# Joined copies and sums over pairs of PSUM banks in a SwiGLU stage on one Trainium2 core

## The chip, the cores and the metric

The kernel runs on one core of one Trainium2 chip. Times are device microseconds (us) of one execution. The profile counts its span from the first to the last instruction, which is a few microseconds less than the device time. Engines: PE is TensorE (matmul; PEld its weight load), ACT is ScalarE, DVE is VectorE, POOL is GpSimd, SP issues most DMAs.

## The reference

Two blocks follow one another, in float32. The first is an attention with sketched features, for 4 batches, 4 heads, 1088 positions and a head size of 32:

```python
def phi(x):
    a = np.einsum('rd,bhsd->bhsr', S1, x)      # r = 8
    b = np.einsum('rd,bhsd->bhsr', S2, x)
    return np.einsum('bhsi,bhsj->bhsij', a, b).reshape(*x.shape[:-1], r * r)
q_p, k_p = phi(q), phi(k)
kv = np.einsum('bhsf,bhsd->bhfd', k_p, v)
z = np.sum(k_p, axis=2)
num = np.einsum('bhsf,bhfd->bhsd', q_p, kv)
den = np.einsum('bhsf,bhf->bhs', q_p, z)[..., None] + 1e-06
```

Its result `num / den`, with the heads laid side by side, is `x` of 4352 tokens by 128. The second block is `g = x @ w_gate`, `silu(g) * (x @ w_val) @ w_out`, with 1536 hidden columns.

## The kernel before, in words

**Tiling.** The tokens lie transposed in `xT` (128 rows, 4352 columns), cut into 12 blocks, three to a batch, of 384, 384 and 320 columns. The hidden columns are 12 chunks of 128. A *unit* `(i, j)` is block `i` and chunk `j`: a gate product, a value product, Silu of the gate, and their product `hj` in one slot of `hbuf`. A *down* product (`down`, L943) then adds `wo` of that chunk times `hj` into the block's accumulator bank, and after the twelfth the block is transposed (`store`, L972) and sent out. The list `todo` keeps the down products five or six units behind.

**Full and cut products.** A full float32 product (L912 in `unit`, L880 for a gate) goes through TensorE in two passes. The units of batches 1 to 3 replace it by three cheaper products of parts (`cut_unit`). Each weight chunk and each token block is split into a coarse part, a scaled fine part and a difference: `w1`, `wb`, `wd` and `x1`, `x0`, `xd` (`cut_weights` L849, `cut_tokens` L859, L860, L864). The product is

```python
d = wd @ xd                                # one bank          L878
p = w1 @ x1 + wb @ x0                      # a second bank     L884, L885
s = (1 + 1/BETA) * p - d / BETA            # ACT L890, then DVE L893
```

The copy on ACT (L890) brings `-d / BETA` from PSUM into an SBUF tile `sum`, and one DVE operation (L893) adds the scaled `p` in place. In a unit with `both` false only the value product is made of parts, and the gate is a full product. In a unit with `both` true gate and value both are: two `d`, two `p`, two L890, two L893, one Silu (L897) that reads the gate's sum, and one GpSimd product (L902).

**Order.** The kernel is written under a manual schedule: each engine runs its instructions in the order in which the code gives them out, and waits on semaphores where data or a buffer isn't there. For a unit of both, ACT's order is copy, copy, Silu, and then the next unit's.

**Stages.** After a head (sketches, batch 0's attention, 36 full units of batch 0, and the first parts of the weights) comes the main loop over `y`, 108 units in the order of `line`: blocks 3, 4, 5, 6, 7, 8, 9, 11, 10, twelve units each, so 384 columns for `y` 0 to 23, 320 for 24 to 35, and so on. Units from `GATES` (22) on are of both; the last unit is a plain `unit`. Between units `parts_of` advances a generator, `attentions()`, which prepares the next batches' attention in pieces. `GROUPS` (6, 8, 22, 24, 40) are the units before which its TensorE pieces run: the numerators of a batch (L760, with copies L777 on ACT and DVE), its key-value sums (L370, and L698 for the key sums `zs`), and the key and query sketches (L336, L324, with copies L572).

**Key sums.** `feature_sums` gives four GpSimd steps (L529) that add up the key features of a batch. For the third batch they were dealt out between the steps of `turn_keys` and `turn_queries` by `beside`, one each.

**Banks.** PSUM has eight banks, `PS`. In the main loop `bank()` takes the one that was used longest ago, except bank 3 (`acc`), which is held for the accumulators. `wide("a")` and `wide("b")` are banks 4, 5 and 6, 7.

Of the kernel before, what the change touches and what calls it, by code (L numbers as in the profile page):

```python
# [7 lines left out]
FP32 = mybir.dt.float32  # L8
# [11 lines left out]
def kernel(  # L20
# [89 lines left out]
    def bank(tag=None):  # L110

        if tag is not None:
            i = place[tag]
        elif oldest[0]:
            i = min((i for i in used if i not in held), key=used.get)
        else:
            i = place[free_banks[turn[0] % len(free_banks)]]
            turn[0] += 1
        touch(i)
        return PS[:, i, :]  # L120

    def wide(tag):
        i = place[tag]
# [418 lines left out]
    def beside(gen, steps):  # L542

        for x in gen:
            if steps:
                steps.pop(0)()
            yield x
# [49 lines left out]
    def attentions():  # L597

        yield from turn_keys(1)
        yield from turn_queries(1)
        hold("a")
        kp = wide("a")
        for i, c in enumerate(kpieces):
            key_products(kp[:, i, :], *c)
        ka = apool.tile([P, NC * H, R], FP32, tag="kas", name="kas")

        def sketch(ps, i):
            c0, c1 = kpieces[i]  # L610
            return ps[:, i, 0 : 64 * (c1 - c0)].rearrange("p (x t r) -> p x t r", t=2, r=R)

        for i, (c0, c1) in enumerate(kpieces):
            nc.scalar.copy(ka[:, H * c0 : H * c1, :], sketch(kp, i)[:, :, 0, :])
        phk = apool.tile([P, NC, H, R, R], FP32, tag="phk", name="phk")
        for n, (i, c0, c1) in enumerate(((0, 0, 3), (0, 3, 5), (1, 5, 7), (1, 7, 9))):
            first = H * (c0 - kpieces[i][0])
            kb = sketch(kp, i)[:, first : first + H * (c1 - c0), 1, :]
            key_features(phk, (ka[:, H * c0 : H * c1, :], kb), c0, c1)
            if n == 3:  # L620
                release("a")
            if n % 3 != 1:
                yield
        zs, sums = feature_sums(phk)
        for f in sums:
            f()
        yield from turn_keys(2)
        kvz = wide("a")
        values(kvz[:, 0, :], phk, zs)
        kab, kcopies = sketched(wide("b"), key_products, 2, "kab2")  # L630
        fold(kvz[:, 0, :])
        spread = spread_out(1, kvz[:, 0, :])
        hold("a", "b")
        yield
        qab, copies = sketched(wide("a"), query_sketches, 3, "qab")
        run_copies(copies, 2)
        yield
        run_copies(kcopies, 2)
        release("a", "b")
        for n, _ in enumerate(query_step(1, qab)):  # L640
            if n % 2 == 0:
                yield
        yield
        yield
        numerators(1, spread)
        yield "first"

        phk = apool.tile([P, NC, H, R, R], FP32, tag="phk", name="phk")
        yield from features(phk, kab)
        zs, sums = feature_sums(phk)  # L650
        yield from beside(turn_keys(3), sums)
        yield from beside(turn_queries(2), sums)
        for b in (2, 3):
            yield "pe"
            if b == 3:
                numerators(2, spread)
            hold("a")
            kv = bank()
            release("a")
            values(kv, phk, zs)  # L660
            if b == 2:
                kab, copies = sketched(wide("a"), key_products, 2, "kab2")
                run_copies(copies, 2)
            fold(kv)
            spread = spread_out(b, kv)
            yield
            yield "pe"
            qab, copies = sketched(wide("b"), query_sketches, 3, "qab")
            run_copies(copies, 2)
            yield  # L670
            if b == 2:
                yield from turn_queries(3)
                phk = hbuf[:, NH - 6 :, :].rearrange("p s (n h i j) -> p (s n) h i j", h=1, i=R, j=R)
                phk = phk.rearrange("p (c h) o i j -> p c (h o) i j", h=H)
                yield from features(phk, kab)
                zs, sums = feature_sums(phk)
            yield from beside(query_step(b, qab), sums)
        yield "pe"
        numerators(3, spread)
        yield  # L680
# [170 lines left out]
    def cut_tokens(i, engine=nc.gpsimd):  # L851
# [14 lines left out]
            op0=ALU.mult, op1=ALU.add,  # L866
        )

    def cut_unit(i, j, both=False):

        t0, n = blocks[i]
        x1, x0, xd = (x[:, 0:n] for x in x_parts[i])
        ws = (wg, wv) if both else (wv,)
        parts = [[x[:, j % 3, :] for x in w_parts[id(w), j // 3]] for w in ws]
        ds = [bank()[:, 0:n] for _ in ws]
        g = None if both else bank()[:, 0:n]
        for d, (_, _, wd) in zip(ds, parts):
            nc.tensor.matmul(d, wd, xd, start=True, stop=True)  # L878
        if not both:
            nc.tensor.matmul(g, wg[:, j, :], xT[:, t0 : t0 + n], start=True, stop=True)  # L880
        ps = []
        for w1, wb, _ in parts:
            p = bank()[:, 0:n]
            nc.tensor.matmul(p, w1, x1, start=True, stop=False)  # L884
            nc.tensor.matmul(p, wb, x0, start=False, stop=True)  # L885
            ps.append(p)
        sums = []
        for d in ds:
            s = fpool.tile([P, BW], FP32, tag="sgl", name="sum", bufs=6)[:, 0:n]
            nc.scalar.activation(s, d, AF.Copy, scale=-1.0 / BETA)  # L890
            sums.append(s)
        for p, s in zip(ps, sums):
            nc.vector.scalar_tensor_tensor(  # L893
                out=s, in0=p, scalar=1.0 + 1.0 / BETA, in1=s, op0=ALU.mult, op1=ALU.add
            )
        sg = fpool.tile([P, BW], FP32, tag="sg", name="sg", bufs=5)[:, 0:n]
        nc.scalar.activation(sg, sums[0] if both else g, AF.Silu)  # L897
        slot_of[i, j] = slots.pop(0)
        hj = hbuf[:, slot_of[i, j], :]
        hidden[i, j] = hj  # L900
        todo.append((i, j))
        nc.gpsimd.tensor_tensor(out=hj[:, 0:n], in0=sg, in1=sums[-1], op=ALU.mult)  # L902

    def unit(i, j, late=False, between=(None, None)):


        t0, n = blocks[i]
        g, u = bank(), bank()
        for o, w in ((g, wg), (u, wv)):
            if between[0] and w is wv:  # L910
                between[0]()
            nc.tensor.matmul(  # L912
                o[:, 0:n], w[:, j, :], xT[:, t0 : t0 + n], start=True, stop=True
            )
        sg = fpool.tile(
            [P, BW], FP32, tag="sgl" if late else "sg", name="sg", bufs=6 if late else 5
        )
        nc.scalar.activation(sg[:, 0:n], g[:, 0:n], AF.Silu)  # L918
        slot_of[i, j] = slots.pop(0)
        hj = hbuf[:, slot_of[i, j], :]  # L920
        hidden[i, j] = hj
        todo.append((i, j))
        if late:
            if between[1]:
                between[1]()
            nc.scalar.copy(hj[:, 0:n], u[:, 0:n])
            lates.append((hj[:, 0:n], sg[:, 0:n]))
        else:
            nc.vector.tensor_tensor(  # L929
                out=hj[:, 0:n], in0=sg[:, 0:n], in1=u[:, 0:n], op=ALU.mult  # L930
            )
# [213 lines left out]
    for z, (i, j) in enumerate(seq):  # L1145
# [16 lines left out]
        if z == 20:  # L1162
            lows = [
                pool.tile([P, 3, P], FP32, tag=tag, name="low", bufs=bufs)[:]
                for pool, tag, bufs in ((apool, "qb", 2), (apool, "dT", 2), (apool, "rd", 2), (fpool, "sgl", 6))
            ]
            first, low, second, third = cut_weights(wv, lows, nc.gpsimd)
        if z in (20, 21):
# [29 lines left out]

    line = [3 * b + k for b in range(1, B) for k in ((0, 2, 1) if b == B - 1 else range(3))]
    END = len(line) * NCH  # L1200
    GROUPS, GATES = (6, 8, 22, 24, 40), 22

    token_steps = {}
    for m, i in enumerate(line[1:], 1):
# [7 lines left out]
    for y in range(END):  # L1212
        i, j = line[y // NCH], y % NCH
        if y in GROUPS:
            group()
        if y == END - 1:
            unit(i, j)
        else:
            cut_unit(i, j, both=y >= GATES)
        for _ in range(2):  # L1220

            if len(todo) > min(5 + (todo[0][1] == 0), END - y + 1):
                down()
        parts_of(y < GATES or y % 2 == 0)
        if y == 0:
            gate_rows = cut_weights(wg, lows, nc.vector)
        for n, row in enumerate(gate_rows):
            if y >= (0, 1, 5, 5)[n]:
                take(row, 1)
        for gen in token_steps.get(y, ()):  # L1230
            next(gen, None)
# [43 lines left out]
```

## Time and profile before

| | us |
|---|---|
| device time, median of 3 runs | 293.69 (293.32 to 293.71) |
| span of the profiled run | 289.9 |
| PE busy | 280.7 (97%) |
| DVE busy | 207.1 (71%) |
| ACT busy | 181.5 (63%) |
| POOL busy | 162.7 (56%) |
| down products L943, 288 | 103.0 |
| copies L890, 192 of them | 80.4 |
| sums L893, 192 of them | 93.9 |
| Silu L897, 85 that read a sum | 42.7 |

The first rows are the whole run, the last four are groups of instructions. "x2" behind a group in the order of time means that two instructions are merged into one line. "Idle before" is an engine's idle time ahead of a group, and the arrow names what ended most of it. The main loop begins at about 92.8 us and the first unit of both has its copies at 140.62 us. The granted clock of TensorE is 1.00 throughout.

### The profile page before, as it was taken

How to read it: one execution, taken by the hardware profiler on the slowest of the kernel's cores; microseconds unless marked ns; L12 is line 12 of the kernel's file. 1: busy time of each engine (PE TensorE's matmuls, PEld its weight loads, DVE VectorE, ACT ScalarE, POOL GpSimd, SP SyncE). 2: the span in 40 equal slices, each digit the busy share in tenths (PEclk: the TensorE clock that was granted, in tenths of full speed). 3: DMA queues.
4: the chain of work that ended last, by engine and by line, in shares of the span. 5: the costliest groups of instructions: out<-in, count | busy, mean ns of one | idle time of the engine just before them, and what ended most of it. 6: DMA issues, size and time to landing. Idle time of an engine off the chain costs nothing.

```text
span 289.9 us, 6382 instructions
## 1 busy us (share of the span) xinstructions
PE 280.7 (97%) x2307; PEld 212.4 (73%) x2307; DVE 207.1 (71%) x422; ACT 181.5 (63%) x432; POOL 162.7 (56%) x183
## 2 busy tenths in 40 slices
PE   8899999999999969999999999999999999999995
PEld 7545566656656657776787768888888888888984
DVE  3997988875677975999578867657666666676651
ACT  3567565732402936564466678887888887888860
POOL 3315322379301794789737665667576665765650
PEclk9999999999999999999999999999999999999999
DMA  7564292312411213001001001001001010010101
GB/s 193 162 209 111 64 308 77 107 49 83 110 18 18 47 65 86 0 1 27 13 6 27 2 0 25 1 0 32 0 0 27 2 24 1 2 27 0 23 2 27
DMA packets 26142, 14.33 MB, mean 49 GB/s; under 512 B 19840, under 2 KB 24192, under 8 KB 26112
## 3 DMA queue, kind: packets, MB, share of 16 engines
q1 hardware_dynamic: 25456, 13.84, 18.4%
q8 instruction: 18, 0.29, 0.4%
q10 hardware_dynamic: 656, 0.10, 0.2%
q14 instruction: 12, 0.10, 0.1%
HBM read 11.41 MB, written 2.23 MB: 47 GB/s over the span
## 4 chain that ended last, share of the span: by engine, by line
PE 84%; DVE 6%; POOL 3%; ACT 2%; issue 2%; DMA 1%; SPq 0%; DVEq 0%; POOLq 0%; ACTq 0%
PE PS L943 26%; PE PS L912 16%; PE PS L884 10%; PE PS L878 10%; PE PS L885 10%; PE PS L880 4%; PE PS L336 2%; PE PS L324 2%; PE PS L760 2%; POOL zs L529 2%; DVE sum L893 1%; DMA kld<-in_k_dram 1%; ACT sum L890 1%; PE PS L370 1%; POOL hbuf L902 1%
## 5 line engine op out<-in xcount | busy, mean ns | idle before, releaser
L902 POOL TENSOR_TENSOR hbuf<-sg,sum 128x384 f32<-128x384 f32 (+1 forms) x107 | 109.4, 1025 | 61.4 <-ACT sg L897 51.2
L893 DVE SCALAR_TENSOR_TENSOR sum<-PS,sum 128x384 f32<-128x384 f32 (+1 forms) x192 | 93.9, 526 | 48.3 <-ACT sum L890 42.1
L943 PE MATMUL PS<-hbuf,wo 128*128 128x384 f32 (+2 forms) x288 | 103.0, 459 | 0.0
L890 ACT ACTIVATE sum<-PS 128x384 f32<-128x384 f32 (+1 forms) x192 | 80.4, 465 | 13.3 <-PE PS L878 12.9
L897 ACT ACTIVATE sg<-sum 128x384 f32<-128x384 f32 (+1 forms) x85 | 42.7, 503 | 27.3 <-DVE sum L893 27.3
L943 PEld LDWEIGHTS PS<-hbuf,wo 128*128 128x128 f32 x288 | 52.0, 189 | 10.3 <-issue 0.4
L878 PE MATMUL PS<-xd,gphq 128*128 128x384 f32 (+1 forms) x85 | 47.9, 564 | 0.0
L884 PE MATMUL PS<-x,w 128*128 128x384 f32 (+1 forms) x107 | 42.2, 394 | 0.1
L878 PE MATMUL PS<-xd,wd 128*128 128x384 f32 (+1 forms) x107 | 39.4, 369 | 0.7 <-DVE sum L893 0.4
L885 PE MATMUL PS<-x,wb 128*128 128x384 f32 (+1 forms) x107 | 35.0, 327 | 0.0
L918 ACT ACTIVATE sg<-PS 128x384 f32<-128x384 f32 (+1 forms) x37 | 17.4, 474 | 22.0 <-PE PS L912 20.3
L912 PE MATMUL PS<-xT,wg 128*128 128x384 f32 (+1 forms) x74 | 29.5, 480 | 0.0
L912 PE MATMUL PS<-xT,wv 128*128 128x384 f32 (+1 forms) x74 | 28.8, 471 | 0.2 <-DVE wv L270 0.2
L878 PEld LDWEIGHTS PS<-xd,wd 128*128 128x128 f32 x107 | 20.3, 189 | 11.5 <-DVE sum L893 1.2
L884 PE MATMUL PS<-x,graw 128*128 128x384 f32 (+1 forms) x85 | 27.9, 328 | 0.0
L885 PE MATMUL PS<-x,graw 128*128 128x384 f32 (+1 forms) x85 | 27.6, 325 | 0.0
L929 DVE TENSOR_TENSOR hbuf<-sg,PS 128x384 f32<-128x384 f32 (+1 forms) x31 | 16.2, 526 | 10.9 <-PE PS L912 10.5
L884 PEld LDWEIGHTS PS<-x,w 128*128 128x128 f32 x107 | 20.1, 188 | 4.2 <-ACT sum L890 0.4
L878 PEld LDWEIGHTS PS<-xd,gphq 128*128 128x128 f32 x85 | 16.1, 189 | 8.6 <-issue 0.4
L885 PEld LDWEIGHTS PS<-x,wb 128*128 128x128 f32 x107 | 20.2, 188 | 2.9
L912 PEld LDWEIGHTS PS<-xT,wv 128*128 128x128 f32 x74 | 13.8, 190 | 9.2 <-DVE hbuf L929 0.9
L912 PEld LDWEIGHTS PS<-xT,wg 128*128 128x128 f32 x74 | 13.3, 189 | 9.3 <-issue 1.2
(130 smaller groups left out, 345.2 us busy)
## 6 DMA issues: line engine op xcount, KB each, us to landing
kld<-in_k_dram SPq DMA_DIRECT2D x4, 544.0 KB, 4.1
vld<-in_v_dram SPq DMA_DIRECT2D x12, 144.0 KB, 4.6
qld<-in_q_dram SPq DMA_DIRECT2D x3, 544.0 KB, 3.3
raw<-in_moe_w_out_dram SPq DMA_DIRECT2D x4, 384.0 KB, 3.8
out_dram<-o SPq DMA_DIRECT2D x28, 48.0 KB, 1.9
raw<-in_moe_w_gate_dram SPq DMA_DIRECT2D x3, 384.0 KB, 3.1
raw<-in_moe_w_val_dram SPq DMA_DIRECT2D x3, 384.0 KB, 3.5
out_dram<-o SPq DMA_DIRECT2D x16, 40.0 KB, 1.7
```

Of the source, the lines that this page charges most:

```text
L878: nc.tensor.matmul(d, wd, xd, start=True, stop=True)
L880: nc.tensor.matmul(g, wg[:, j, :], xT[:, t0 : t0 + n], start=True, stop=True)
L884: nc.tensor.matmul(p, w1, x1, start=True, stop=False)
L885: nc.tensor.matmul(p, wb, x0, start=False, stop=True)
L890: nc.scalar.activation(s, d, AF.Copy, scale=-1.0 / BETA)
L893: nc.vector.scalar_tensor_tensor(out=s, in0=p, scalar=1.0 + 1.0 / BETA, in1=s, op0=ALU.mult, op1=ALU.add)
L897: nc.scalar.activation(sg, sums[0] if both else g, AF.Silu)
L902: nc.gpsimd.tensor_tensor(out=hj[:, 0:n], in0=sg, in1=sums[-1], op=ALU.mult)
L912: nc.tensor.matmul(o[:, 0:n], w[:, j, :], xT[:, t0 : t0 + n], start=True, stop=True)
L918: nc.scalar.activation(sg[:, 0:n], g[:, 0:n], AF.Silu)
L929: nc.vector.tensor_tensor(out=hj[:, 0:n], in0=sg[:, 0:n], in1=u[:, 0:n], op=ALU.mult)
L943: nc.tensor.matmul(acc[i][:, 0:n], wo[:, j, :], hidden[i, j][:, 0:n], start=(j == 0), stop=(j == NCH - 1),)
```

## The change

The change has four parts.

1. A new `pair()` takes two neighbouring banks at once. A unit of both puts its two `d` on one pair and its two `p` on another, so that one ACT copy and one DVE sum of 2 x 384 (or 2 x 320) columns take the place of two each. `doubles` gives the sum tiles: tiles of two halves, four buffers, in place of six single ones. This is for fewer instructions on ACT and DVE.
2. `GATES` goes from 22 to 18: four more units make the gate of parts too. The rate of `parts_of` keeps its limit of 22.
3. The key sums of the third batch are given out in one go, ahead of `turn_keys(3)`, and the first two `GROUPS` come at units 5 and 7 in place of 6 and 8, so that TensorE reaches the values a unit earlier.
4. The gate weights' later rows are cut a unit later, and the fourth low part of the value weights lies in a buffer of tag `qb`, since `sgl` has another shape now.

```diff
+    def pair():
+        i = min((i for i in (0, 4, 6) if i not in held), key=lambda i: max(used[i], used[i + 1]))
+        touch(i, i + 1)
+        return PS[:, i : i + 2, :]
...
         zs, sums = feature_sums(phk)
-        yield from beside(turn_keys(3), sums)
-        yield from beside(turn_queries(2), sums)
+        for f in sums:
+            f()
+        yield from turn_keys(3)
+        yield from turn_queries(2)
...
+    room = [None, 2]
+    def doubles(k):
+        if room[1] + k > 2:
+            room[:] = fpool.tile([P, 2, BW], FP32, tag="sgl", name="sum", bufs=4), 0
+        at = room[1]
+        room[1] += k
+        return room[0][:, at : at + k, :]
...
-        ds = [bank()[:, 0:n] for _ in ws]
+        ds = pair()[:, :, 0:n] if both else bank()[:, 0:n].unsqueeze(1)
         g = None if both else bank()[:, 0:n]
-        for d, (_, _, wd) in zip(ds, parts):
-            nc.tensor.matmul(d, wd, xd, start=True, stop=True)
+        for k, (_, _, wd) in enumerate(parts):
+            nc.tensor.matmul(ds[:, k], wd, xd, start=True, stop=True)
...
-        ps = []
-        for w1, wb, _ in parts:
-            p = bank()[:, 0:n]
-            nc.tensor.matmul(p, w1, x1, start=True, stop=False)
-            nc.tensor.matmul(p, wb, x0, start=False, stop=True)
-            ps.append(p)
-        sums = []
-        for d in ds:
-            s = fpool.tile([P, BW], FP32, tag="sgl", name="sum", bufs=6)[:, 0:n]
-            nc.scalar.activation(s, d, AF.Copy, scale=-1.0 / BETA)
-            sums.append(s)
-        for p, s in zip(ps, sums):
-            nc.vector.scalar_tensor_tensor(
-                out=s, in0=p, scalar=1.0 + 1.0 / BETA, in1=s, op0=ALU.mult, op1=ALU.add
-            )
+        ps = pair()[:, :, 0:n] if both else bank()[:, 0:n].unsqueeze(1)
+        for k, (w1, wb, _) in enumerate(parts):
+            nc.tensor.matmul(ps[:, k], w1, x1, start=True, stop=False)
+            nc.tensor.matmul(ps[:, k], wb, x0, start=False, stop=True)
+        sums = doubles(len(ws))[:, :, 0:n]
+        nc.scalar.activation(sums, ds, AF.Copy, scale=-1.0 / BETA)
+        nc.vector.scalar_tensor_tensor(
+            out=sums, in0=ps, scalar=1.0 + 1.0 / BETA, in1=sums, op0=ALU.mult, op1=ALU.add
+        )
         sg = fpool.tile([P, BW], FP32, tag="sg", name="sg", bufs=5)[:, 0:n]
-        nc.scalar.activation(sg, sums[0] if both else g, AF.Silu)
+        nc.scalar.activation(sg, sums[:, 0] if both else g, AF.Silu)
...
-    GROUPS, GATES = (6, 8, 22, 24, 40), 22
+    GROUPS, GATES = (5, 7, 22, 24, 40), 18
...
-        parts_of(y < GATES or y % 2 == 0)
+        parts_of(y < 22 or y % 2 == 0)
...
-            if y >= (0, 1, 5, 5)[n]:
+            if y >= (0, 2, 6, 6)[n]:
                 take(row, 1)
```

More of the change, by code (lines that the diff above doesn't have):

```diff
@@ L901, in cut_unit @@
         todo.append((i, j))
-        nc.gpsimd.tensor_tensor(out=hj[:, 0:n], in0=sg, in1=sums[-1], op=ALU.mult)
+        nc.gpsimd.tensor_tensor(out=hj[:, 0:n], in0=sg, in1=sums[:, len(ws) - 1], op=ALU.mult)
     def unit(i, j, late=False, between=(None, None)):
@@ L914, in unit @@
             )
-        sg = fpool.tile(
-            [P, BW], FP32, tag="sgl" if late else "sg", name="sg", bufs=6 if late else 5
-        )
+        sg = doubles(1)[:, 0, :] if late else fpool.tile([P, BW], FP32, tag="sg", name="sg", bufs=5)
         nc.scalar.activation(sg[:, 0:n], g[:, 0:n], AF.Silu)
@@ L1164 @@
                 pool.tile([P, 3, P], FP32, tag=tag, name="low", bufs=bufs)[:]
-                for pool, tag, bufs in ((apool, "qb", 2), (apool, "dT", 2), (apool, "rd", 2), (fpool, "sgl", 6))
+                for pool, tag, bufs in ((apool, "qb", 2), (apool, "dT", 2), (apool, "rd", 2), (apool, "qb", 2))
             ]
```

## The prediction

> **What bounds the kernel now.** I read the page's busy line first, then the chain that ended last, then the last stage by form and in order of time.
>
> The busy line and the chain:
>
> ```profile
> PE 280.7 (97%) x2307; PEld 212.4 (73%) x2307; DVE 207.1 (71%) x422; ACT 181.5 (63%) x432; POOL 162.7 (56%) x183
> ...
> PE 84%; DVE 6%; POOL 3%; ACT 2%; issue 2%; DMA 1%; SPq 0%; DVEq 0%; POOLq 0%; ACTq 0%
> ```
>
> The reader is to see that TensorE is busy nearly throughout and owns the end. ScalarE at 63% looks like an engine with room. The next two views show why that is not so.
>
> The groups by form between 175 and 285 us (busy, mean ns, idle before and its releaser):
>
> ```profile
> L893 DVE SCALAR_TENSOR_TENSOR sum<-PS,sum 128x384 f32<-128x384 f32 x86 | 44.0, 553 | 24.0 <-ACT sum L890 23.6
> ...
> L890 ACT ACTIVATE sum<-PS 128x384 f32<-128x384 f32 x86 | 37.2, 485 | 0.3 <-PE PS L878 0.2
> ...
> L897 ACT ACTIVATE sg<-sum 128x384 f32<-128x384 f32 x43 | 22.6, 526 | 12.5 <-DVE sum L893 12.5
> L893 DVE SCALAR_TENSOR_TENSOR sum<-PS,sum 128x320 f32<-128x320 f32 x48 | 21.3, 486 | 11.6 <-ACT sum L890 11.4
> ...
> L890 ACT ACTIVATE sum<-PS 128x320 f32<-128x320 f32 x48 | 18.2, 431 | 0.1
> ```
>
> Each engine of a unit waits for the other: the sums for the copies, the Silu for the sums. The copies wait for almost nothing, so they start when the Silu ahead of them in ScalarE's queue is done.
>
> One turn of that ring, in order of time, where nothing else disturbs it (start, length):
>
> ```profile
> 169.97 0.85 ACT L890 ACTIVATE sum<-PS 128x384 f32<-128x384 f32 x2
> ...
> 170.47 1.02 DVE L893 SCALAR_TENSOR_TENSOR sum<-PS,sum 128x384 f32<-128x384 f32 x2 [0.50 <-ACT sum L890]
> ...
> 171.07 0.52 ACT L897 ACTIVATE sg<-sum 128x384 f32<-128x384 f32 x1 [0.24 <-DVE sum L893]
> 171.50 0.85 ACT L890 ACTIVATE sum<-PS 128x384 f32<-128x384 f32 x2
> ```
>
> First copy to first sum 0.50 us, first sum to Silu 0.60, Silu to the next unit's copy 0.43: 1.53 us a turn. The second copy runs beside the first sum, and the second sum beside the Silu. For 320 columns the same reading (copies at 150.08, sums at 150.53, Silu at 151.06, copies at 151.43) gives 0.45 + 0.53 + 0.37 = 1.35.
>
> TensorE in the steady part, the second difference product of two successive units:
>
> ```profile
> 184.55 0.34 PE L878 MATMUL PS<-xd,wd 128*128 128x384 f32 x1
> ...
> 186.25 0.34 PE L878 MATMUL PS<-xd,wd 128*128 128x384 f32 x1
> ```
>
> That is 1.70 us a unit (six products 0.17 apart and a down product of 0.65). TensorE sets the time with 0.17 us to spare over the ring. This margin is what the change must not use up.
>
> Earlier, the one real hole in TensorE, from the waits between 100 and 106 us:
>
> ```profile
> PE PS L698 <- POOL zs L529: 2.3, 1, 2.3
> ```
>
> The third batch's key sums reach TensorE late.
>
> **What the Trainium skill says.** PSUM — Partial Sum Buffer, section "Engine vs sequencer instructions": the queues of ScalarE, VectorE and GpSimd are strictly first in, first out. The trace agrees: before the Silu at 149.70 ScalarE stood idle for 1.56 us on a sum, with the next unit's copies behind it. ScalarE: Activation LUTs, "What ACT_TABLE_LOAD costs": 186 ns + 0.833 ns per element for an ACTIVATE with immediate scale, successive ones overlapping by about 93 ns. At 384 that is 506 ns against 485 here. VectorE: DVE Perf Modes, section on the TRN2 errata: 120 cycles and one per element from PSUM at 0.96 GHz, 525 ns at 384 against 553 here. So both engines pay mostly per element, and joining two operations saves only the fixed part.
>
> **The change part by part.**
>
> *Joined copies and sums.* No instruction with 768 elements from PSUM is in the trace. From the two widths, L890 costs (485 - 431)/64 = 0.84 ns per column and L893 (553 - 486)/64 = 1.05. So 384 more columns add 0.32 us to the copy (0.81) and 0.40 to the sum (0.95); 320 more add 0.27 and 0.335. The skill's prices give estimates of 0.83 and 0.93 for 768. From above, a joined operation should cost no more than the two that it replaces (0.85 and 1.02). I take 0.81 and 0.95.
> Per unit this saves about 0.04 us of ScalarE and 0.07 of VectorE, but it puts both halves in series. The gate's sum can't start before the value's copy is done, and the Silu can't start before the value's sum is done. The new wait is the Silu's: behind it on ScalarE stands the next unit's joined copy, for which the next sum, and then the PSUM pair, and then TensorE wait. The ring becomes, at 384: 0.50 + 0.32 = 0.82 to the sum, 0.60 + 0.40 = 1.00 to the Silu, 0.43 to the next copy: 2.25 us. At 320: 0.72 + 0.87 + 0.37 = 1.96. TensorE's 1.70 no longer hides it.
>
> *Pairs of banks.* A unit of both takes two of three pairs where seven single banks turned before. The next difference products wait for the sum of two products back, which ended before; the next value products wait for the joined copy. Both come ahead of ScalarE's turn in the ring, so I cost this at nothing: the ring hides it.
>
> *How many turns.* Units 18 to 105 start 88 periods: 52 at 384 and 36 at 320 (blocks of 12 units; 18 to 23 at 384, then 12 at 320, 24 at 384, 12 at 320, and so on): 52 x 2.25 + 36 x 1.96 = 187.6 us.
> To that come ScalarE's other work and TensorE's groups, hidden before and now in the ring: six token copies (L859) at 0.42, 2.5 us; the group at unit 22, where the numerators (1.56 us on TensorE) wait for unit 21's sum, and then values, a copy of 0.70 and the next products follow, 5.35 instead of 2.25, 3.1 us; the query sketches at 24 (1.67 us on TensorE, ScalarE copies of 1.14) 1.2; the denominator chain on VectorE (147.14 to 149.18, five operations, against some 1.1 us free) 0.8; the numerators at unit 40, 2.0; single turns where two other VectorE operations of 0.5 and 0.95 meet, 0.7. In all 10.3 us. Alone, an operation of 0.95 fits in VectorE's gap of 1.1 to 1.3.
> Before, first copy of unit 18 to that of unit 106 took 279.08 - 129.67 = 149.4 us. Change: 187.6 + 10.3 - 149.4 = +48.5 us.
>
> *Gates from 18.* Four units take six short products in place of three and a full gate product. On TensorE that would save 4 x (1.82 - 1.70) = 0.5 us (1.82 is the distance of units at 121 to 128 us). In the ring it costs 4 x 0.43; the +48.5 holds it.
>
> *Key sums at once, groups at 5 and 7.* Before, the sums on GpSimd (1.3, 1.3, 1.0, 0.9 us) stand between units' products and end at 104.1. In one go they start when the third batch's features are done (94.3) and end at about 98.8. A group one unit earlier reaches them after its key products at about 99.9, so the wait of 2.3 us goes. The units' products queue behind the sums, some 2.7 us later at unit 0; their down products come seven units on, which hides that. I take -2.3 us, between -0.5 and -2.8.
>
> *Gate rows a unit later, GATES split from the 22 of the attention parts, another home for the fourth low part, the doubled sum tiles.* Nothing: the rows were done by about unit 10, and the low part's old contents are dead some 10 us before the next tokens are cut.
>
> *Tail.* Before, 10.8 us from unit 106's copy to the end, TensorE with a backlog. After, TensorE has none: 3.4 us to the last GpSimd product, 2.4 of down and last products, 3.4 for copy and transfer out, 9.2. So -1.6.
>
> Sum: 48.5 - 2.3 - 1.6 = +44.6 us; 293.7 + 44.6 = 338.3, so 338 us.
>
> **The rivals.**
> *TensorE stays the bound* (6%). For it: the chain is 84% TensorE, ScalarE idles 37% of the span, and fewer, longer operations save fixed cost. The time would be 293.7 - 2.3 - 0.5 = 290.9 us, faster. Against it: a ring of 1.70 us would need the joined copy and sum to take about what single ones take.
> *The ring lengthens by about half* (6%): if joined operations take 0.65 and 0.7 us, the period is some 1.9 and 1.65, 158 + 8 - 149 = +17, less 4: 307 us. Against it: both slopes, measured over 128 and more instructions.
> *TensorE's clock falls* (5%). TensorE: Matmul & The Clock Gate, "What's actually happening": half clock after an idle window of about 3.4 us. TensorE would idle 0.55 us of each 2.25, never 3.4 but at the groups; the trace shows 1.00 throughout. At half clock a unit costs 3.4 at 384 and 2.8 at 320, 52 x 3.4 + 36 x 2.8 = 278, +127: about 417 us.
>
> **How the numbers follow.** The ring as worked out, 83%: 338 us. If joining saves nothing, the turns are 2.37 and 2.07, +10; if they are 0.1 shorter, -9. The extras may be 5 to 16. Together 324 to 352 holds 8 in 10. Slower takes the ring, the half case and the clock, 94%; faster 5%, the first rival with part lost to no change, 1%.
>
> **What would show it.** Right: one L890 and one L893 a unit at 768 columns, near 0.81 and 0.95; the Silu idling about 1.0 us on the sum each unit; L897 starts 2.25 apart at 384 and 1.96 at 320; TensorE near 75% busy after 135 us, waiting for L893 or L890; the chain then mostly ScalarE and VectorE; no wait of L698 for L529. Wrong: L897 starts 1.7 apart, copies of a later unit ahead of a Silu on ScalarE, or a granted clock below 1.

## The result, and the profile after

The changed kernel takes 338.99 us (338.66 to 339.18) against 293.7: a ratio of 1.152, 95% interval 1.144 to 1.159. The profiled span grows from 289.9 to 336.9 us. Runs of one kernel differ by about 1.5 us, some of them before the main loop starts (its first copy begins at 93.2 to 93.8 us in most traces, at 94.8 and 95.1 in two) and some with TensorE's granted clock (last section), so below the stretch from that copy to the end is given beside the time: 196.7 us before, 243.7 after.

In the changed file the copies are L904, the sums L905, the Silu L909, the GpSimd products L914, the down products L953, the value products L901 and L902. From the page of after, the busy line and the chain:

```profile
PE 301.4 (89%) x2311; PEld 209.9 (62%) x2311; DVE 204.7 (61%) x337; ACT 173.4 (51%) x347; POOL 160.0 (47%) x183
...
PE 34%; DVE 29%; ACT 19%; issue 13%; POOL 2%; DMA 1%; POOLq 0%; SPq 0%; DVEq 0%; ACTq 0%
```

VectorE and ScalarE have 85 instructions fewer each and less to do, 2.4 and 8.1 us, and all engines have a smaller share of the span. TensorE no longer owns the end. A busy matmul row also holds time in which it waits: it shows 301.4 us for 2311 matmuls against 280.7 for 2307, though after replaces four full gate products by cheaper ones.

The groups by form of after, 175 to 320 us:

```profile
L905 DVE SCALAR_TENSOR_TENSOR sum<-PS,sum 128x768 f32<-128x768 f32 x43 | 41.2, 957 | 52.0 <-ACT sum L904 50.8 <-PE PS L902 1.3
L904 ACT ACTIVATE sum<-PS 128x768 f32<-128x768 f32 x43 | 34.1, 793 | 0.0
...
L909 ACT ACTIVATE sg<-sum 128x384 f32<-128x384 f32 x43 | 22.5, 523 | 44.4 <-DVE sum L905 44.4
```

The joined copy takes 0.793 us and the joined sum 0.957. The Silu's idle time goes from 12.5 us for 43 units to 44.4, 1.03 a unit. One turn of the chain of after, in order of time (start, length, what):

```profile
199.39 0.80 ACT sum L904
200.19 0.02 issue
200.22 0.97 DVE sum L905
201.18 0.02 issue
201.21 0.02 ACT sg L909
201.23 0.41 issue
201.63 0.80 ACT sum L904
```

This is the whole ring: copy, sum, Silu, and the next copy right behind the Silu on ScalarE. 201.63 - 199.39 = 2.24 us, with no TensorE in it.

### The profile page after: what moved, and what is told of

It reads as the page before. It is cut to its first block, busy times and chain, and to the rows that moved or that the text cites. A ratio compares the mean times of both kernels' runs of the same rounds, so it can differ in the third digit from the quotient of the medians.

```text
span 336.9 us, 6038 instructions
## 1 busy us (share of the span) xinstructions
PE 301.4 (89%) x2311; PEld 209.9 (62%) x2311; DVE 204.7 (61%) x337; ACT 173.4 (51%) x347; POOL 160.0 (47%) x183
## 4 chain that ended last, share of the span: by engine, by line
PE 34%; DVE 29%; ACT 19%; issue 13%; POOL 2%; DMA 1%; POOLq 0%; SPq 0%; DVEq 0%; ACTq 0%
DVE sum L905 23%; ACT sum L904 17%; PE PS L924 13%; PE PS L953 8%; PE PS L330 1%; PE PS L901 1%; PE PS L898 1%; DMA kld<-in_k_dram 1%; POOL zs L535 1%; PE PS L902 1%; PE PS L342 1%; PE PS L768 1%; PE PS L896 1%; ACT x L867 1%; PE PS L376 1%
## 5 line engine op out<-in xcount | busy, mean ns | idle before, releaser
L914 POOL TENSOR_TENSOR hbuf<-sg,sum 128x384 f32<-128x384 f32 (+1 forms) x107 | 106.9, 1003 | 111.2 <-ACT sg L909 100.9
L905 DVE SCALAR_TENSOR_TENSOR sum<-PS,sum 128x768 f32<-128x768 f32 (+2 forms) x107 | 89.9, 841 | 99.6 <-ACT sum L904 93.0
L953 PE MATMUL PS<-hbuf,wo 128*128 128x384 f32 (+2 forms) x288 | 103.3, 460 | 0.9 <-POOL hbuf L914 0.9
L909 ACT ACTIVATE sg<-sum 128x384 f32<-128x384 f32 (+1 forms) x89 | 44.6, 502 | 91.8 <-DVE sum L905 91.8
L904 ACT ACTIVATE sum<-PS 128x768 f32<-128x768 f32 (+2 forms) x107 | 75.6, 707 | 9.5 <-PE PS L896 9.3
L901 PE MATMUL PS<-x,graw 128*128 128x384 f32 (+1 forms) x89 | 37.2, 418 | 25.3 <-ACT sum L904 24.6
L953 PEld LDWEIGHTS PS<-hbuf,wo 128*128 128x128 f32 x288 | 51.9, 189 | 11.8 <-POOL hbuf L914 1.5
L896 PE MATMUL PS<-xd,gphq 128*128 128x384 f32 (+1 forms) x89 | 50.1, 563 | 1.2 <-DVE sum L905 1.0
L901 PEld LDWEIGHTS PS<-x,graw 128*128 128x128 f32 x89 | 16.6, 187 | 48.2 <-ACT sum L904 47.1
L901 PE MATMUL PS<-x,w 128*128 128x384 f32 (+1 forms) x107 | 40.5, 379 | 0.1
L896 PE MATMUL PS<-xd,wd 128*128 128x384 f32 (+1 forms) x107 | 38.2, 357 | 0.2 <-DVE xd L872 0.2
L902 PE MATMUL PS<-x,wb 128*128 128x384 f32 (+1 forms) x107 | 35.0, 327 | 0.0
L902 PE MATMUL PS<-x,graw 128*128 128x384 f32 (+1 forms) x89 | 29.0, 326 | 0.0
L896 PEld LDWEIGHTS PS<-xd,wd 128*128 128x128 f32 x107 | 20.3, 190 | 10.2 <-issue 0.7
L928 ACT ACTIVATE sg<-PS 128x384 f32<-128x384 f32 (+1 forms) x31 | 14.3, 465 | 21.4 <-PE PS L924 19.6
L896 PEld LDWEIGHTS PS<-xd,gphq 128*128 128x128 f32 x89 | 16.8, 189 | 13.4 <-DVE sum L905 5.0
L939 DVE TENSOR_TENSOR hbuf<-sg,PS 128x384 f32<-128x384 f32 (+1 forms) x31 | 16.2, 525 | 10.3 <-PE PS L924 9.0
L901 PEld LDWEIGHTS PS<-x,w 128*128 128x128 f32 x107 | 20.1, 188 | 2.8 <-DVE sum L905 0.4
L902 PEld LDWEIGHTS PS<-x,wb 128*128 128x128 f32 x107 | 20.1, 188 | 2.4
```

The costliest lines, as they stand in the source:

```text
L896: nc.tensor.matmul(ds[:, k], wd, xd, start=True, stop=True)
L901: nc.tensor.matmul(ps[:, k], w1, x1, start=True, stop=False)
L902: nc.tensor.matmul(ps[:, k], wb, x0, start=False, stop=True)
L904: nc.scalar.activation(sums, ds, AF.Copy, scale=-1.0 / BETA)
L905: nc.vector.scalar_tensor_tensor(out=sums, in0=ps, scalar=1.0 + 1.0 / BETA, in1=sums, op0=ALU.mult, op1=ALU.add)
L909: nc.scalar.activation(sg, sums[:, 0] if both else g, AF.Silu)
```

## The experiments

Each table row gives the median time, the ratio to before with its 95% interval, and the stretch from the loop's first copy to the end of the trace.

| kernel | us | ratio | loop to end |
|---|---|---|---|
| before | 293.2 to 293.7 | 1 | 196.7 |
| after | 338.99 | 1.152 (1.144 to 1.159) | 243.7 |
| e1, split operations on pairs | 292.04 | 0.998 (0.997 to 0.999) | 196.4 |
| e2, copy joined | 307.87 | 1.051 (1.047 to 1.055) | 212.4 |
| e3, sum joined | 348.91 | 1.190 (1.186 to 1.193) | 253.5 |
| e4, both joined, late Silu | 291.74 | 0.995 (0.994 to 0.997) | 196.5 |
| e5, before with the new head | 290.71 | 0.993 (0.991 to 0.995) | 195.3 |
| e6, before with gates from 18 | 294.92 | 1.007 (1.004 to 1.010) | 199.6 |
| e7, after with gates from 22 | 340.13 | 1.162 (1.157 to 1.167) | 244.2 |
| e8, split, late Silu, gates from 18 | 293.12 | 1.000 (0.998 to 1.003) | 196.5 |
| e9, e4 with gates from 22 | 293.52 | 1.003 (1.001 to 1.004) | 198.2 |
| e10, e5 with late Silu | 288.46 | 0.985 (0.982 to 0.989) | 193.2 |

**Is it the joining, or the pairs of banks?** e1 keeps the pairs and splits both operations again:

```diff
-        nc.scalar.activation(sums, ds, AF.Copy, scale=-1.0 / BETA)
+        for k in range(len(ws)):
+            nc.scalar.activation(sums[:, k], ds[:, k], AF.Copy, scale=-1.0 / BETA)
-        nc.vector.scalar_tensor_tensor(
-            out=sums, in0=ps, scalar=1.0 + 1.0 / BETA, in1=sums, op0=ALU.mult, op1=ALU.add
-        )
+        for k in range(len(ws)):
+            nc.vector.scalar_tensor_tensor(
+                out=sums[:, k], in0=ps[:, k], scalar=1.0 + 1.0 / BETA, in1=sums[:, k],
+                op0=ALU.mult, op1=ALU.add,
+            )
```

> The kernel after, with two copies and two sums a unit again, on the same pairs of banks. Theory of the ring (joining puts both halves in series): a turn is back to 1.53 us at 384 columns and 1.35 at 320, below TensorE's 1.70, so 289 to 294 us. Rival (the coarse hand-over of three pairs of banks is what costs): TensorE still waits for pairs each unit, and the time stays above 315 us.

292.04 us: the loss is gone with the pairs still there. The rival falls.

**Which of the two?** e2 takes over only the second half of that edit (the sum is split, the copy joined), e3 only the first (the copy is split, the sum joined).

> The kernel after, with the copy joined and the sum split. Ring: 0.82 + 0.60 + 0.43 = 1.85 us at 384, 0.72 + 0.53 + 0.37 = 1.62 at 320, which is 33 us less than joined sums over 88 turns: 303 to 310 us. Rival (each joining gives half of the loss): about 316 us.

> The kernel after, with the copy split and the sum joined. Ring: the joined sum waits for the second of two copies, 0.89 + 1.00 + 0.43 = 2.32 us at 384 and 0.79 + 0.87 + 0.37 = 2.03 at 320, so no better than the kernel after: 339 to 346 us. Rival (each joining gives half of the loss): about 316 us.

e2 took 307.87, inside the ring's range and 8 us below the rival. A turn of e2 in order of time:

```profile
195.04 1.02 DVE L906 SCALAR_TENSOR_TENSOR sum<-PS,sum 128x384 f32<-128x384 f32 x2 [0.82 <-ACT sum L904]
...
195.64 0.53 ACT L911 ACTIVATE sg<-sum 128x384 f32<-128x384 f32 x1 [0.62 <-DVE sum L906]
196.07 0.79 ACT L904 ACTIVATE sum<-PS 128x768 f32<-128x768 f32 x1
...
196.89 1.02 DVE L906 SCALAR_TENSOR_TENSOR sum<-PS,sum 128x384 f32<-128x384 f32 x2 [0.82 <-ACT sum L904]
```

The sums come 1.85 us apart, as worked out: the Silu starts 0.60 after the first of the two. e3 took 348.91, slower than the kernel after, as the ring says and the rival can't. It also missed its range, by 3 us. Its chain shows why:

```profile
209.29 0.86 ACT sum L905 x2
210.15 0.04 DVEq L906
210.19 0.04 issue
210.23 0.97 DVE sum L906
...
211.66 0.86 ACT sum L905 x2
```

From the first copy's start to the joined sum it is 0.94 us, where I had 0.89: two copies take 0.86 to the end of the second, and 0.08 pass before the sum starts. A turn is 2.37 and not 2.32, 4 us over 88 turns.

The same trace shows that TensorE has no part in the ring. Its granted clock is 0.50 from 271.3 to 274.7 us, and the turns keep their length; three Silus in order of time:

```profile
270.27 0.52 ACT L910 ACTIVATE sg<-sum 128x384 f32<-128x384 f32 x1 [1.08 <-DVE sum L906]
...
272.64 0.52 ACT L910 ACTIVATE sg<-sum 128x384 f32<-128x384 f32 x1 [1.08 <-DVE sum L906]
...
275.00 0.52 ACT L910 ACTIVATE sg<-sum 128x384 f32<-128x384 f32 x1 [1.08 <-DVE sum L906]
```

They are 2.37 and 2.36 us apart. So most of the loss comes with the joined sum, and with it in place a joined copy is better than two.

**Is it the joined operations, or the order on ScalarE?** e4 keeps everything of after and moves one thing: the Silu and the GpSimd product of a unit of both are given out after the next unit's copy. `finish` gives out the two, `settle` those that wait; it is also called ahead of the last unit.

```diff
         nc.scalar.activation(sums, ds, AF.Copy, scale=-1.0 / BETA)
+        settle()
...
-        nc.scalar.activation(sg, sums[:, 0] if both else g, AF.Silu)
-        nc.gpsimd.tensor_tensor(out=hj[:, 0:n], in0=sg, in1=sums[:, len(ws) - 1], op=ALU.mult)
+        waiting.append(finish)
```

> The kernel after with copies and sums joined and pairs of banks kept, but a unit's Silu and its GpSimd product are given out after the next unit's copy. Ring: ScalarE no longer holds the next copy behind the Silu's wait, so joined operations cost nothing and TensorE is the bound again: 286 to 293 us, with Silus about 1.7 us apart at 384. Rival (joined operations or pairs of banks are slow in themselves): above 315 us.

291.74 us, with the same joined instructions. In order of time, e4:

```profile
184.70 0.51 ACT L916 ACTIVATE sg<-sum 128x384 f32<-128x384 f32 x1
184.83 0.96 DVE L906 SCALAR_TENSOR_TENSOR sum<-PS,sum 128x768 f32<-128x768 f32 x1 [0.63 <-ACT sum L904]
185.68 0.81 ACT L904 ACTIVATE sum<-PS 128x768 f32<-128x768 f32 x1 [0.47 <-PE PS L896]
186.39 0.51 ACT L916 ACTIVATE sg<-sum 128x384 f32<-128x384 f32 x1
```

The Silu now waits for nothing, the copy waits for TensorE, and Silus are 1.69 us apart: TensorE's own pace. So the 47 us are neither the joined operations alone (e4 has them) nor this order alone (e1 and before have it with split operations): the two together make the ring. This is the experiment that settles the cause. What joining costs once the order is mended is seen from e8 to e10.

**The head alone.** e5 is the kernel before with the key sums in one go, groups at 5 and 7 and the later gate rows.

> The kernel before with the third batch's key sums in one go, groups at 5 and 7 and the later gate rows, and nothing else. If the wait of 2.3 us on the key sums was on the path: 1.5 to 2.5 us less than before, 290.8 to 291.8. Rival (the time comes back as a wait further on, for the sketch or the gate rows): within 0.6 us of before.

290.71 us. The median is 2.5 us lower than that of before, but the trace is only 1.4 us shorter from the loop's first copy: about half of the executions of before have a lower mean clock and take some 1.6 us more, and none of e5's does (last section). Against the executions of before at a mean clock of 1.00, which have a median of 292.0, e5 gains 1.3. The rival, that the time comes back in full, falls; a part does come back (below).

**The four units more of both.** e6 makes them in the kernel before, e7 takes them out of the kernel after.

> The kernel before with units of both from 18 on, and nothing else. If TensorE is the bound there: 0.5 us less than before (four full gate products of 0.65 become three products of 0.17). Rival (VectorE, nearly full at 120 to 130 us, takes four more sums of 0.55 late): 0 to 2 us more than before.

> The kernel after with units of both from 22 on again. Ring: four turns of 2.25 become four units of 1.82, so 1.7 us less than after; and the wait of 4.1 us of unit 18's Silu, which the trace of after shows behind VectorE's attention work, goes or shrinks, up to 2.5 us more: 334.5 to 337.5 us. Rival (gates of parts help even in the ring): 339 or more.

In e6 the rival was right: 1.7 us slower. The traces differ by 2.9, but 1.6 of that is there from unit 6 on, long before unit 18, where e6's clock falls after the wait on the key sums (last section); the rest, 1.3, comes between units 18 and 22. VectorE lags behind attention work there; its waits between 130 and 140 us begin with

```profile
ACT sg L897 <- DVE sum L893: 3.6, 2, 2.4
```

which the kernel before doesn't have in that stretch. In a plain-gate unit the Silu reads the gate from PSUM and doesn't wait for VectorE; in a unit of both it does.

e7 missed its expectation: 340.13, and 244.2 us from the loop's first copy against 243.7, so no gain at all. Its first copy of unit 22 comes 2.7 us earlier than in after, counted from the loop's first copy (46.25 against 48.96), but two units later the lead is 0.3. Waits of e7 between 137 and 153 us:

```profile
PE PS L330 <- DVE sum L905: 1.1, 1, 1.1
DVE sum L905 <- PE PS L902: 1.1, 1, 1.1
...
PE PS L901 <- DVE spread L716: 1.0, 1, 1.0
```

The value products of unit 22 got a pair of which one bank was still read by the transpose of the key-value sums. And the query sketches at unit 24 (L330) wait for a joined sum. After has neither wait. Together they are 2.1 us, against a lead that shrinks by 2.4; that they are the whole cause was not tried alone.

**Joining with the order mended.** e8 is e5 with gates from 18 and the late Silu, so split operations on single banks; e9 is e4 with gates from 22. The edits are those of e4 and one number.

> The kernel before with the head of e5, units of both from 18 on, single banks with split copies and sums, and the Silu and product of a unit of both given out after the next unit's copies. If order alone matters and joining is neither good nor bad once the Silu is late: within 1 us of e4 (291.7), 290.5 to 292.5. Rival (joined operations relieve ScalarE and VectorE in the stretch where VectorE is nearly full): e4 is faster by more than 1 us.

> e4 with units of both from 22 on: joined copies and sums, pairs of banks, late Silu. If the four early units of both cost what they cost alone (e6, +1.75 us) here too: 289.5 to 291 us. Rival (the late Silu hides VectorE's lag at 18 to 21): within 0.5 us of e4, 291.2 to 292.2.

e8 took 293.12, 0.6 us above its range. By the medians its rival holds, since e4 is 1.4 us faster. But 12 of e8's 22 executions have a mean clock of 0.994 or less, and the other ten a median of 292.05, in the range and 0.3 from e4; e8's trace is late before the loop, and from the loop's first copy e8 and e4 both need 196.5 us. So in these traces joining is worth nothing either way; whether split operations bring the lower clock stays open.

e9 missed: 293.52, slower than e4. Waits of e9 between 137 and 153 us:

```profile
PE PS L896 <- DVE sum L906: 1.1, 1, 1.1
PE PS L901 <- DVE spread L716: 1.0, 1, 1.0
PE PS L330 <- DVE sum L906: 0.6, 1, 0.6
```

The difference products (L896) wait as long in e4. The other two are e7's, and e4 has neither, nor a wait of 0.7 of the numerators at unit 40 on a joined sum. So pairs are not free where a group of single banks meets them. These three waits are 2.3 us, against a loss of 1.7 in the loop; that they are its cause was not tried alone.

**A version that beats both.** e10 is e5 with the late Silu, split operations, single banks, gates from 22.

> e5 with the Silu and product of a unit of both given out after the next unit's copies; split operations, single banks, units of both from 22 on. If ScalarE's order still costs in the stretch from 145 to 170 us, where the ring waits for VectorE: 1 to 2.5 us less than e5 (290.7), 288.2 to 289.7. Rival (that stretch is bound by VectorE's own work, not by the order): within 0.7 us of e5.

288.46 us, ratio 0.985 (0.982 to 0.989) to before, 2.2 us less than e5 and 50.5 less than after. Between 150 and 160 us, windows of before and of e10 (from, to, length, then busy us of PE, PEld, DVE, ACT, POOL, granted clock, DMA share and GB/s):

```profile
150.00:160.00 10.00, 9.88 (x51) 7.84 (x49) 8.18 (x17) 7.24 (x20) 7.27 (x7) 1.00 0.13 22
```

```profile
150.00:160.00 10.00, 10.00 (x56) 8.64 (x55) 10.00 (x21) 8.14 (x23) 7.61 (x8) 1.00 0.14 22
```

In the same 10 us e10 gets 56 matmuls through in place of 51 (e5, in the old order, 50) and VectorE is full: the ring had cost the kernel before something too, wherever VectorE's attention work sat in it. The rival falls.

e9 and e10 also make a pair that differs in joining alone, with its pairs of banks and the buffers that go with them: both have the new head, gates from 22 and the late Silu. They are level up to unit 21 (its copy comes 41.3 us after the loop's first in both), and then e9 needs 198.2 us to the end against 193.2. So where e4 and e8 are level, e9 is 5.0 us slower than e10: joining was not free once the order was mended. Beside a wait of 0.9 on the transpose that both have, TensorE waits 3.4 us in e9 for joined sums and for L716 at or just behind the groups, and 0.5 us in e10 for a sum. The rest of the 5.0 is open, and no run tells joined operations from pairs of banks here.

## Why the prediction was right, point by point

**The ring** was the step that carried it, and it held to 0.01 us: 2.25 and 1.96 forecast, 2.24 and 1.95 measured (Silus at 201.21 and 203.45; at 232.47 and 234.42). The terms were right as well: joined copy 0.81 forecast and 0.79 measured, joined sum 0.95 and 0.96. The estimates from the Trainium skill's prices (ScalarE: Activation LUTs, "What ACT_TABLE_LOAD costs", and VectorE: DVE Perf Modes, the TRN2 errata), 0.83 and 0.93, were each 0.03 off; the slopes of the trace were nearer. The reading that mattered was not ScalarE's busy share (63%) but which instruction stands behind the one that waits. e4 shows it: the same instructions in another order, 47 us less. One sign was off: TensorE was to be near 75% busy after 135 us and shows 168.0 of the 195 us from 135 to 330, 86%.

**The other work in the ring** was put at 10.3 us, and first copy of unit 18 to first copy of unit 106 took 326.39 - 127.96 = 198.4 us against 197.9 forecast. The total fits because errors cancelled. ScalarE of after in order of time:

```profile
127.96 0.81 ACT L904 ACTIVATE sum<-PS 128x768 f32<-128x768 f32 x1
132.89 0.53 ACT L909 ACTIVATE sg<-sum 128x384 f32<-128x384 f32 x1 [4.12 <-DVE sum L905]
```

The first Silu of both waited 4.12 us and not 1.02, since VectorE, with attention work before it, began unit 18's sum 3.1 us after the copy's end (131.85 against 128.77). I hadn't foreseen these 3.1 us. In return the group at unit 22 cost 2.0 and not 3.1 (copies at 137.93 and 142.19), the sketches 0.8 and not 1.2, the numerators at 40 about 1.0 and not 2.0. The denominators cost 1.2 and not 0.8.

**Pairs of banks at nothing**: right for the change as made (e1, and turns of after as long as the ring). e7 and e9 show that it isn't general: 1.0 us at unit 22 when a pair meets a bank of a group.

**Gates from 18**, put at +1.7 in the ring: not shown. e7 gave nothing back (243.7 against 244.2). Taken alone they cost the kernel before 1.7 us (e6), for another reason, VectorE's lag.

**The head** at -2.3: unit 18's copy came 1.7 us earlier (127.96 against 129.67), and e5 gained 1.4 in its trace. The wait of L698 on the key sums is gone from the waits, as forecast. What came in its place, in the waits of after between 84 and 120 us:

```profile
PE PS L898 <- DVE spread L716: 0.9, 1, 0.9
```

An earlier group also moves the next unit's gate product up to the transpose that it has to wait for. Net of that, e5 leads before by 2.0 us at unit 8 (Silus, counted from the loop's first copy), and by 1.2 from unit 19 on; 0.4 of what it loses between is a wait of the down products on the transpose of a finished block.

**The tail** was mis-sized: -1.6 forecast, -0.3 measured (10.5 us from unit 106's copy to the end, where I had worked out 9.2).

The traces' sum is 49.0 - 1.7 - 0.3 = 47.0 us, 336.9 - 289.9. The medians differ by 45.3, since the profiled run of before, 291.78 us, is one of its shorter ones, at a clock of 1.00 throughout. The prediction took its terms from that trace and added them to the longer median, 293.7; so its 44.6 is 2.4 short of what the terms came to, and that 338.3 lands within 0.7 of 338.99 is in part luck.

**The rivals.** TensorE as the bound needed a ring of 1.70 us with early Silus: it was 2.24. The half case needed joined operations of 0.65 and 0.7. The clock stayed at 0.998 to 1.000 in the four runs of after, and e3's turns kept their length where it fell.

## What to carry to other kernels

- Look for rings: an engine that runs in order, waits for a second engine, and has behind that wait the instruction which the second engine needs next. The ring's period is the sum of its parts and their hand-overs, however idle each engine looks; joining two short operations into one long one lengthens it by the half that used to overlap (here from 1.53 us to 1.85 with the joined copy and 2.25 with both).
- Before merging or splitting instructions, break the ring by order: give out the waiting instruction after the next unit's independent one. That was worth 47 us here with joined operations and some 2 us with split ones. Joining then gained nothing: level in one pair of kernels (e4, e8), 5 us slower in the other (e9, e10), so the split kernel is the better one to keep.
- A unit that brings a busy engine into an in-order chain (VectorE in the gate's path, e6) pays that engine's backlog at once; look at what its queue holds at the place, not at the average.

## What the runs showed that was not expected

Splitting the copy in two delays a joined sum by 0.11 us a unit (0.94 from the first copy's start against 0.83 for the joined copy), which over 88 turns is nearly all of the 9.9 us by which e3 is slower than after.

The clock is the other surprise. In e6's trace TensorE waits 2.3 us for the key sums, and right behind that wait, from 104.8 to 108.2 us, the granted clock is 0.50; the trace of before has the same wait and a clock of 1.00. From the next Silu on e6 is 1.6 us behind before, each counted from its loop's first copy. Of the 33 executions of before taken beside e5, 16 have a mean clock of 1.000 and take 291.7 to 292.2 us, and 17 have 0.994 or less and take 293.2 to 295.0. In e5, where TensorE's longest wait there is 0.9 us, all nine have 0.998 or more (of e10, with the same head, one of six has 0.994). So closing the hole seems to bring a second gain beside the wait itself, and a gap of 2.3 us, which the prediction's clock rival did not look at, may be enough for the fall. Only e6's trace shows where the clock fell, though, and no run here tells why it falls in some executions and not in others.
